# A causal mask added by products, head pairs reduced together, and fill products in blocks of twelve: one change to a fused attention and two-layer MoE kernel

## The chip, the core and the metric

The kernel runs on one core of one Trainium2 chip. The metric is the device time of one execution in microseconds (us). The engines are TensorE (PE, and PEld for its weight loads), VectorE (DVE), ScalarE (ACT), GpSimd (POOL) and SyncE (SP, which issues all the DMAs here).

## The reference, cut to what matters

```python
scores = scale * np.matmul(q, k.transpose(0, 1, 3, 2))     # batch 4, 8 heads, 576 tokens, head_dim 64
cum = np.cumsum(np.log(np.clip(f, 0.0001, 1.0)), axis=-1)
scores = np.where(causal, -1000000000.0, scores + cum[:, :, :, None] - cum[:, :, None, :])
scores = scores - np.max(scores, axis=-1, keepdims=True)
attn = np.exp(scores)
attn = attn / (np.sum(attn, axis=-1, keepdims=True) + 1e-09)
x = np.matmul(attn, v)                 # then 2304 tokens x 512
h = x @ w_in                           # 512 x 2048
x = (np.maximum(h, 0.0) + alpha * np.minimum(h, 0.0)) @ w_out
h2 = x @ w_in2
out = (h2 * np.tanh(softplus(h2))) @ w_out2
```

The weights are float64; the kernel turns them into float32 itself. The row maximum is taken over causal keys only.

## The kernel before, in words

**Order.** Nothing runs in the order of the source. Each piece of work is registered with `plan.add(engine, cost, priority, function, reads, writes)`, and `Plan.emit` then lists all of it, with estimated costs, and writes out one fixed order for each engine. An engine takes its instructions strictly in that order, so one that waits holds up all behind it. The table `PRIO` shifts starting priorities by stage name and by the number of the operation within its stage. A "use" (`plan.use`) is a PSUM buffer that the planner picks from a group: the group "two" has three pairs of banks, the group "one" has the single bank 6 before the change. The fill (below) has bank 7.

**Attention.** 32 heads go through as 16 pairs; the two heads of a pair lie in partitions 0 to 63 and 64 to 127, and their products run beside each other on two halves of TensorE (tile 64*128). For each pair:

- `load_qk`, `load_v`, `load_bias`: DMAs. `stage_T` splits q and k into a high and a low float32r part (ACT cast, then DVE subtraction, L331).
- `stage_M` (maxima): for five chunks of 128 queries, in six pieces of 320, 256, 64, 448, 320 and 192 keys, a q-k product (L609) and a bias product (L611) for each head go into a pair of banks. Then DVE takes, for each head by itself, the maximum with the mask `tri` added (L619, twelve operations per pair of heads, each followed by the reading of its accumulator) into `M5`. The five 128x128 columns of `M5` are transposed on TensorE (L631), and ACT adds `bvec` and writes `BQ` (L636, two operations).
- `stage_S` (scores): four pieces, each four passes (three q-k passes, and a last one with `BQ` and `BK` that adds bias and minus the maximum; L657). ACT takes the exponential (L667), POOL zeroes the upper triangle (L675).
- `stage_R` (row sums): POOL adds blocks (L693), TensorE sums over keys (L705), ACT and DVE form the reciprocal `uu` (L710 to L717).
- `stage_V`: products with v (L738) in two windows, and DVE scales them into `X` (L744).

`stage_S` of a pair stands one step behind `stage_M` in the source, so several pairs are in flight.

**Fill.** `group_a` computes part of the first MoE layer for three blocks of 384 tokens while attention is still running: four hidden chunks with 12 products of 128x384 each (`h_mm`, L782 to L784), the activation (`prelu`), and four output chunks with 12 products each (`out1`, L847 to L849). That is 288 products. Before the change the planner may place them in threes. `load_w` brings the eight weight tiles for it: a DMA, then ACT and DVE conversions (L399 to L405), and a split (ACT, POOL L331).

**The rest.** When attention is through, its memory is given back (`swap1`), and the remaining MoE work runs to the end, with 512-column products at L858 to L860.

Of the kernel before, what the change touches and what calls it, by code (L numbers as in the profile page):

```python
# [9 lines left out]
F32 = mybir.dt.float32  # L10
F32R = mybir.dt.float32r
# [226 lines left out]
def fox_attention__then__moe_prelu__then__moe_mish(  # L238
# [53 lines left out]
    banks = {n: psum.tile([P, 512], F32, tag=f"b{n}", name=f"b{n}") for n in range(8)}  # L292
# [115 lines left out]
    def conv_w(l, kind, fc, at, after=()):  # L408

        src = ((w_in1, w_out1), (w_in2, w_out2))[l][kind]  # L410
        i = n_w[0] % 2 if n_w[0] >= 2 * GA else 0
        n_w[0] += 1
        wbk = [("wb", i, m) for m in range(2)]
        for m in range(2):
            half_w(src, kind, fc, i, m, at, after if i else ())
        return lambda: wbs[i].bitcast(F32), wbk
# [6 lines left out]
    def load_w(l, kind, fc, slot, at, after=()):  # L423
        plan.stage("W" if after else "WA")
        split_w(*conv_w(l, kind, fc, at, after), (slot, kind), at, after)
# [31 lines left out]
    KEEP = 4  # L457
    PRE = "DVE"
    W_AT = 0.0
    bM = [7]  # L460
# [4 lines left out]
    plan.share("two", [(banks[2 * n], banks[2 * n + 1]) for n in range(3)])  # L465
    plan.share("one", [banks[6]])
# [13 lines left out]
    Pt = [ap1.tile([P, 2, PW], F32, tag=f"Pt{i}", name=f"Pt{i}") for i in range(2)]  # L480
# [5 lines left out]
    M5 = [ap1.tile([P, NQ, P], F32, tag=f"M5{i}", name=f"M5{i}") for i in range(2)]  # L486
# [3 lines left out]
    rr = ap1.tile([P, S], F32, tag="rr", name="rr")  # L490
    uu = ap1.tile([P, S], F32, tag="uu", name="uu")
    tri = ap1.tile([P, S + P], F32, tag="tri", name="tri")
    junk = ap1.tile([P, S - P], F32, tag="junk", name="junk")
    BQ1 = ap1.tile([P, P], F32R, tag="BQc", name="BQc")
    bvec = ap1.tile([P, 1], F32, tag="bvec", name="bvec")
# [4 lines left out]
    bias = c1[:NH, 2 * S:5 * S].rearrange("p (t n) -> p t n", t=3)  # L500

# [5 lines left out]
    def bank(group):  # L507
        n = bank_use.get(group[0], 0)
        bank_use[group[0]] = n + 1
        b = group[n % len(group)]  # L510
        return banks[b], ("bank", b)
# [6 lines left out]
    def prologue():  # L518
# [5 lines left out]
        plan.add("DVE", 0.74, -27, lambda: V.memset(tri, 0.0), w=["zero"])  # L524
        plan.add("POOL", 0.24, -25, lambda: G.affine_select(
            out=tri[:, S:], in_=tri[:, S:], pattern=[[-1, P]], compare_op=ALU.is_ge, fill=NEG, base=0, channel_multiplier=1),
            ["zero"], ["tri"])
        plan.add("POOL", 0.6, -12, lambda: G.memset(bias[:, 1], 1.0), r=pk, w=["bias1"])
        plan.add("DVE", 0.5, -9, lambda: V.tensor_scalar(fr, fr, 1e-4, 1.0, op0=ALU.max, op1=ALU.min), ["f"] + pk, ["f1"])
        plan.add("ACT", 0.67, -9, lambda: nc.scalar.activation(fr, fr, AF.Ln), ["f1"] + pk, ["f2"])  # L530
        plan.add("DVE", 0.8, -9, lambda: V.tensor_tensor_scan(
            out=cum, data0=fr, data1=tri[:NH, :S], initial=0.0, op0=ALU.add, op1=ALU.add), ["f2", "zero"] + pk, ["cum"])
# [3 lines left out]
            out=bias[:, 2].bitcast(F32R), in0=cum, scalar=m8, in1=bias[:, 0], op0=ALU.mult, op1=ALU.subtract), ["bh", "cum"] + pk, ["bl"])  # L536
        plan.add("DVE", 0.5, -20, lambda: (V.memset(bvec, 0.0), [V.memset(bvec[e * HALF:e * HALF + 3], 1.0) for e in range(2)]), w=["bvec"])
        plan.add("DVE", 0.5, -19, lambda: (V.memset(BQ1.bitcast(F32), 0.0), [V.memset(BQ1[e * HALF:e * HALF + 3].bitcast(F32), 1.0) for e in range(2)]), w=["BQ1"])
        plan.add("POOL", 0.3, -10, lambda: (G.memset(ones, 1.0), G.memset(eps, 1e-9)), w=["ones"])
        for i in range(2):  # L540
            plan.add("POOL", 0.7, -18 + 9 * i, lambda i=i: G.memset(BK[i].bitcast(F32), 0.0), w=[("BK", i)])
            plan.add("POOL", 0.7, -17 + 9 * i, lambda i=i: G.memset(M5[i], 0.0), w=[("M5", i, c) for c in range(NQ)])
# [27 lines left out]
    def load_v(pr, at):  # L570
        plan.stage("LV2")
        i = pr % 2
        n4 = (NQ - 1) * P
        dma(at, lambda: nc.sync.dma_start(vt[i][:, :NQ - 1], v[pr, :n4].rearrange("(c p) x -> p c x", p=P)), 262, runs=1.3, w=[("v", i, 0)])
        dma(at, lambda: nc.sync.dma_start(vt[i][:HALF, NQ - 1], v[pr, n4:]), 33, r=[("vpad", i)], w=[("v", i, 1)], issue=0.62)
# [11 lines left out]

    hs = [slice(e * HALF, (e + 1) * HALF) for e in range(2)]

    def stage_M(pr, at):  # L590
# [4 lines left out]
        for c in [NQ - 1, 0] + list(range(NQ - 2, 0, -1)):  # L595
# [5 lines left out]
            for n, (a, z) in enumerate(pieces):  # L601
# [5 lines left out]
                def mm(ps=ps, a=a, z=z, q0=q0):  # L607
# [430 lines left out]
```

## Time and profile before

| What | Value |
|---|---|
| Device time, three runs | median 1064.71 us (1062.28 to 1065.77) |
| The profiled execution | 1062.31 us, span 1060.5 us |
| Granted TensorE clock, mean | 0.985 |
| PE busy / DVE busy | 1023.7 us (97%) / 770.8 us (73%) |
| ACT busy / POOL busy | 520.0 us (49%) / 421.8 us (40%) |
| Last attention operation (L744) ends | 294.4 us |

A busy PE is not a PE at its peak: products are pipelined, each row's duration is longer than the distance to the next one, and an engine that runs at half the clock counts as busy too. What a product costs is therefore read from start to start in the timeline.

### The profile page before, as it was taken

How to read it: one execution, taken by the hardware profiler on the slowest of the kernel's cores; microseconds unless marked ns; L12 is line 12 of the kernel's file. 1: busy time of each engine (PE TensorE's matmuls, PEld its weight loads, DVE VectorE, ACT ScalarE, POOL GpSimd, SP SyncE). 2: the span in 40 equal slices, each digit the busy share in tenths (PEclk: the TensorE clock that was granted, in tenths of full speed). 3: DMA queues.
4: the chain of work that ended last, by engine and by line, in shares of the span. 5: the costliest groups of instructions: out<-in, count | busy, mean ns of one | idle time of the engine just before them, and what ended most of it. 6: DMA issues, size and time to landing. Idle time of an engine off the chain costs nothing.

```text
span 1060.5 us, 17610 instructions
## 1 busy us (share of the span) xinstructions
PE 1023.7 (97%) x6332; PEld 922.4 (87%) x6332; DVE 770.8 (73%) x1686; ACT 520.0 (49%) x1101; POOL 421.8 (40%) x416
## 2 busy tenths in 40 slices
PE   7897899999989999999999999999999999999998
PEld 6665677777779999999999999998999999999997
DVE  6776876766478877878622247979888788887885
ACT  3544555545346554534332336645455555554543
POOL 2554563554545654414232334333243322423231
PEclk9988999999989999999999999999999999999999
DMA  6132322210033445665510024100000000000000
GB/s 184 56 97 76 88 67 58 69 42 19 12 101 99 125 143 162 203 192 191 188 31 1 20 80 130 49 1 31 1 1 30 1 31 1 1 31 1 31 1 30
DMA packets 55207, 70.86 MB, mean 67 GB/s; under 512 B 6576, under 2 KB 32176, under 8 KB 55120
## 3 DMA queue, kind: packets, MB, share of 16 engines
q1 hardware_dynamic: 55120, 69.75, 21.5%
q8 instruction: 49, 0.80, 0.3%
q14 instruction: 38, 0.31, 0.1%
HBM read 56.39 MB, written 13.33 MB: 66 GB/s over the span
## 4 chain that ended last, share of the span: by engine, by line
PE 81%; DVE 9%; DMA 4%; issue 3%; ACT 1%; SPq 0%; POOL 0%; DVEq 0%; ACTq 0%
PE b L782 11%; PE b L784 11%; PE b L783 11%; PE b L859 6%; PE b L858 6%; PE b L860 6%; PE b L657 5%; PE b L847 5%; PE b L738 5%; PE b L849 4%; PE b L848 4%; DVE junk L619 2%; PE b L609 2%; DVE wb L405 2%; DVE wb L403 2%
## 5 line engine op out<-in xcount | busy, mean ns | idle before, releaser
L782 PE MATMUL b<-xh,w 128*128 128x384 f32 x768 | 260.5, 339 | 3.5 <-DVE x L807 1.3
L784 PE MATMUL b<-xl,w 128*128 128x384 f32 x768 | 257.8, 336 | 4.8 <-DVE xl L331 4.8
L783 PE MATMUL b<-xh,w 128*128 128x384 f32 x768 | 257.4, 335 | 0.0
L839 POOL TENSOR_TENSOR x<-x 128x384 f32<-128x384 f32 x96 | 113.0, 1177 | 245.5 <-DVE x L837 165.9
L782 PEld LDWEIGHTS b<-xh,w 128*128 128x128 f32 x768 | 144.1, 188 | 13.5 <-issue 2.2
L784 PEld LDWEIGHTS b<-xl,w 128*128 128x128 f32 x768 | 144.3, 188 | 5.2 <-DVE xl L331 5.2
L783 PEld LDWEIGHTS b<-xh,w 128*128 128x128 f32 x768 | 144.2, 188 | 3.9
L847 PE MATMUL b<-g,w 128*128 128x384 f32 x384 | 132.6, 345 | 8.0 <-DVE x L810 7.2
L331 POOL TENSOR_TENSOR g<-X,g 128x384 fp32r<-128x384 f32 x72 | 78.2, 1090 | 155.3 <-ACT g L321 124.2
L849 PE MATMUL b<-g,w 128*128 128x384 f32 x384 | 129.9, 338 | 0.0
L848 PE MATMUL b<-g,w 128*128 128x384 f32 x384 | 129.7, 338 | 0.0
L321 ACT CAST g<-x 128x384 fp32r<-128x384 f32 x120 | 61.6, 513 | 112.9 <-POOL x L839 103.8
L860 PE MATMUL b<-w,g 128*128 128x512 f32 x288 | 113.1, 393 | 0.0
L859 PE MATMUL b<-w,g 128*128 128x512 f32 x288 | 113.1, 393 | 0.0
L858 PE MATMUL b<-w,g 128*128 128x512 f32 x288 | 113.0, 392 | 0.0
L807 DVE SCALAR_TENSOR_TENSOR X<-X,alph,b 128x384 f32<-128x384 f32 x72 | 43.8, 610 | 74.5 <-ACT X L801 74.2
L619 DVE CUSTOM_DVE_ANT_0 junk<-b,tri 128x320 f32<-128x320 f32 (+3 forms) x160 | 69.2, 432 | 33.6 <-PE b L611 15.9
L331 DVE TENSOR_TENSOR g<-x,g 128x384 fp32r<-128x384 f32 x102 | 75.5, 742 | 16.9 <-ACT g L321 16.7
L399 ACT ACTIVATE wb<-raw 128x256 f32<-128x256 f32 x128 | 52.5, 433 | 69.0 <-DMA wd<-wb 33.8
L847 PEld LDWEIGHTS b<-g,w 128*128 128x128 f32 x384 | 73.1, 190 | 12.5 <-DVE x L810 8.4
L667 ACT ACTIVATE Pt<-b 128x512 f32<-128x512 f32 (+1 forms) x128 | 57.1, 505 | 42.8 <-PE b L657 41.5
L401 DVE TENSOR_SCALAR wb<-wb 128x256 int32<-128x256 int32 x128 | 54.5, 443 | 31.6 <-ACT wb L399 30.9
(94 smaller groups left out, 1999.4 us busy)
## 6 DMA issues: line engine op xcount, KB each, us to landing
raw<-in_moe_w_in_dram SPq DMA_DIRECT2D x64, 256.0 KB
raw<-in_moe_w_out_dram SPq DMA_DIRECT2D x64, 256.0 KB
wd<-wb SPq DMA_DIRECT2D x32, 256.0 KB
raw<-wd SPq DMA_DIRECT2D x32, 256.0 KB
qkr<-in_q_dram SPq DMA_DIRECT2D x16, 288.0 KB
qkr<-in_k_dram SPq DMA_DIRECT2D x16, 288.0 KB
out_dram<-x SPq DMA_DIRECT2D x18, 256.0 KB
vt<-in_v_dram SPq DMA_DIRECT2D x16, 256.0 KB
```

The source lines that it names most:

```text
L331: plan.add(engs, 0.0, at, lambda e: (nc.gpsimd if e == "POOL" else nc.vector).tensor_tensor(out=out(), in0=in0(), in1=in1(), op=ALU.subtra ...
L619: nc.vector.tensor_tensor_reduce(out=junk[ql, :z - a], in0=ps()[e][ql, :z - a], in1=tri[ql, x0 + a:x0 + z], scale=-1.0, scalar=BIG if n == ...
L782: nc.tensor.matmul(ps[:, :NB], w[:, 0, c], xh[c], start=(c == 0), stop=False)
L783: nc.tensor.matmul(ps[:, :NB], w[:, 1, c], xh[c], start=False, stop=False)
L784: nc.tensor.matmul(ps[:, :NB], w[:, 0, c], xl[c], start=False, stop=(c == KC - 1))
L839: add("POOL", c_pool(NB, 2.2), lambda e, m: nc.gpsimd.tensor_tensor(out=m, in0=e, in1=m, op=ALU.mult), [ek, mk], [mk])
L847: nc.tensor.matmul(ps[:, :NB], w[:, 0, c], g[:, 0], start=first, stop=False)
L848: nc.tensor.matmul(ps[:, :NB], w[:, 1, c], g[:, 0], start=False, stop=False)
L849: nc.tensor.matmul(ps[:, :NB], w[:, 0, c], g[:, 1], start=False, stop=last)
L858: nc.tensor.matmul(ps, g[:, 0, sl], w[:, 0], start=first, stop=False)
L859: nc.tensor.matmul(ps, g[:, 0, sl], w[:, 1], start=False, stop=False)
L860: nc.tensor.matmul(ps, g[:, 1, sl], w[:, 0], start=False, stop=last)
```

## The change

The change does these things.

- **Mask.** In the last piece of each chunk, four more products per piece (L635 of the changed kernel: two halves of the mask for each head, a 64x128 selector `sel` against a 64-row part of `tri`) add the causal mask in PSUM. `tri` shrinks to 128 columns; the prologue builds `sel` and `tri`.
- **Maxima.** One DVE `tensor_reduce` (L643) takes the maxima of both heads of a piece out of a double bank; `M5` is now 128 x 10 and one TensorE transpose (L650) of ten columns follows. ACT writes it, negated, as ten rows `MT` (L652), and four small DMAs on SP's queue (L656) move these rows into `BQ`. `bvec` and `junk` are gone.
- **Fill.** When the fill's bank group is given as a name, `h_mm` and `group_a` register twelve products as one operation, so nothing can be placed between them. The fill and `stage_V` now share the group "one", which has banks 6 and 7.
- **Loads.** The first weight loads come one pair later and wait for a `BQ` DMA of that pair; the order of the eight tiles is four w_in, then four w_out; the first v load waits for the first bias load.
- **Buffers.** `rr` and `uu` are doubled, and the first half of the reciprocal is written back into PSUM.

```diff
+    pairs = [pairs_pool.tile([P, 2, 512], F32, tag=f"bb{n}", name=f"bb{n}") for n in range(3)]
...
-    plan.share("two", [(banks[2 * n], banks[2 * n + 1]) for n in range(3)])
-    plan.share("one", [banks[6]])
+    plan.share("two", pairs)
+    plan.share("one", [banks[6], banks[7]])
...
-    M5 = [ap1.tile([P, NQ, P], F32, tag=f"M5{i}", name=f"M5{i}") for i in range(2)]
+    M5 = [ap1.tile([P, 2, NQ], F32, tag=f"M5{i}", name=f"M5{i}") for i in range(2)]
+    MT = [ap1.tile([2 * NQ, P], F32R, tag=f"MT{i}", name=f"MT{i}") for i in range(2)]
...
     def stage_M(pr, at):
...
                     for e in range(2):
-                        nc.tensor.matmul(ps()[e][:, :z - a], BQ1[hs[e]], BK[i][hs[e], a:z], start=False, stop=True)
+                        nc.tensor.matmul(ps()[:, e, :z - a], BQ1[hs[e]], BK[i][hs[e], a:z], start=False, stop=not last)
+                    if last:
+                        w = z - max(q0, a)
+                        for half in range(2):
+                            for e in range(2):
+                                nc.tensor.matmul(ps()[:, e, z - a - w:z - a], sel[hs[e], half], tri[hs[e], half, :w], start=False, stop=half == 1)
...
-                for e in range(2):
-                    dst = lambda e=e, c=c, ql=ql: M5[i][ql, c, e * HALF + 1:e * HALF + 2]
-                    plan.add("DVE", c_dve(z - a) * 1.08 + 0.01, ai, lambda e=e, ps=ps, a=a, z=z, ql=ql, n=n, last=last, x0=x0, dst=dst:
-                             nc.vector.tensor_tensor_reduce(
...
+                plan.add("DVE", c_dve(2 * (z - a)), ai, lambda ps=ps, a=a, z=z, ql=ql, dst=dst: nc.vector.tensor_reduce(
+                    out=dst(), in_=ps()[ql, :, :z - a], axis=mybir.AxisListType.X, op=ALU.max), [bk], ["nmx"] if part else [("M5", i, c)])
...
-        def tr():
-            for c in range(NQ):
-                q0 = rows(c)[0]
-                half = int(q0 >= W0)
-                nc.tensor.transpose(ps()[half][:, q0 - half * W0:q0 - half * W0 + P], M5[i][:, c], ident)
...
+        plan.add("PE", 0.11, at + 6, lambda: nc.tensor.transpose(ps()[:2 * NQ, 0, :P], M5[i].rearrange("p e c -> p (e c)"), ident),
+                 ["ident"] + [("M5", i, c) for c in range(NQ)], [bk, ("MT", i)])
+        plan.add("ACT", c_act(P), at + 6.3, lambda: nc.scalar.activation(MT[i], ps()[:2 * NQ, 0, :P], AF.Copy, scale=-1.0), [bk], [("MT", i)])
+        for e in range(2):
+            for c, n in ((0, 1), (1, NQ - 1)):
+                q0, w = rows(c)
+                dma(at + 6.5, lambda e=e, c=c, n=n, q0=q0, w=w: nc.sync.dma_start(
+                    BQ[i][e * HALF + 1:e * HALF + 2, q0:q0 + n * w].bitcast(F32),
+                    MT[i][e * NQ + c:e * NQ + c + n, :w].bitcast(F32)),
+                    2, r=[("MT", i), ("BQ1", i)], w=[("BQ", i, e, min(c, 1))], issue=0.62)
...
     def h_mm(slot, bs, at):
...
-        for c in range(KC):
...
-            plan.add("PE", 3 * c_pe(NB), at, mm, [("wh",) + wk, ("wl",) + wk, ("xh", c), ("xl", c)], [bk])
+        for cs in [range(KC)] if whole else [[c] for c in range(KC)]:
+            plan.add("PE", 3 * len(cs) * c_pe(NB), at, lambda cs=cs: mm(cs),
...
-                if h < 2 * GA:
-                    load_w(0, h % 2, h // 2, h // 2, at + (h % 2) * II + W_AT)
+                h -= 2 * W_FROM
+                if 0 <= h < 2 * GA:
+                    load_w(0, h // GA, h % GA, h % GA, at + (h % 2) * II + W_AT, behind=[("BQ", pr % 2, 0, 0)])
...
-        group_a(blk, TF0 + blk * 2 * GA * TFS, TFS, bM)
+        group_a(blk, TF0 + blk * 2 * GA * TFS, TFS, "one")
```

**Where the order moves: TensorE, transposes and scores.** Before, the five transposes of a pair's maxima (`M_134`, here pair 2) stand behind the row sums (L705), and the maxima of the next pair (L609, L611) follow.

```order
L705 MATMUL b_67<-Pt_122,ones 64x128 x2
L705 MATMUL b_67<-accp,ones 64x160 x2
L705 MATMUL b_68<-accp,ones 64x288 x2
L631 MATMUL b_69<-ident,M_134 128x128 x3
L631 MATMUL b_70<-ident,M_134 128x128 x2
L609 MATMUL b_65<-khl_129,qhl_127 128x320
L609 MATMUL b_66<-khl_129,qhl_127 128x320
```

In the changed kernel the maxima of pairs 2 and 3 come first, all of them with the mask products (L635); then the single transpose of pair 2 (`M_137`), the row sums (L725), the transpose of pair 3 (`M_138`), and at once the scores of pair 2 (L677), whose last pass reads `BQ_135`.

```order
L628 MATMUL bb_70<-khl_132,qhl_130 128x192 x2
L630 MATMUL bb_70<-BK_134,BQc 128x192 x2
L635 MATMUL bb_70<-tri,sel 128x128 x4
L650 MATMUL bb_68<-ident,M_137 10x128
L725 MATMUL bb_68<-Pt_125,ones 64x128 x2
L725 MATMUL bb_68<-accp,ones 64x160 x2
L725 MATMUL bb_68<-accp,ones 64x288 x2
L650 MATMUL bb_69<-ident,M_138 10x128
L677 MATMUL bb_70<-qhl_129,khl_131 128x288 x6
L677 MATMUL bb_70<-BQ_135,BK_133 128x288 x2
```

So between a pair's transpose and the first use of its `BQ` there stand here six row-sum products and one transpose.

**Where the order moves: SP's queue.** Before, SP's first thirty rows hold input, bias, v and weight loads; a stretch of it, where `raw` is the landing place of the weights, `BK` the bias rows and `qkr` the next pair's q and k:

```order
L566 DMA BK_131<-biasd 3x576 x2
L389 DMA raw_91<-in_moe_w_in_dram 128x2x128 x2
L393 DMA raw_91<-in_moe_w_out_dram 128x256 x2
L566 DMA BK_130<-biasd 3x576 x2
L389 DMA raw_91<-in_moe_w_in_dram 128x2x128
L558 DMA qkr_124<-in_k_dram 128x576
```

In the changed kernel the eight `BQ` DMAs of pairs 0 and 1 (L656) stand there, ahead of the first weight load, of the bias of pair 2 and of the next q and k loads.

```order
L656 DMA BQ_136<-MT_140 1x16x4
L656 DMA BQ_136<-MT_140 1x4x128
L656 DMA BQ_136<-MT_140 1x16x4
L656 DMA BQ_136<-MT_140 1x4x128
L393 DMA raw_94<-in_moe_w_in_dram 128x2x128 x2
L586 DMA BK_133<-biasd 3x576 x2
```

Over the whole program SP's rows grow by the four `BQ` DMAs of each of the 16 pairs.

## Rows read from the trace of the kernel before

**Rows 1.** The page's first line: span and instructions.

```profile
span 1060.5 us, 17610 instructions
```

**Rows 2.** Busy time by stage: length, PE, PEld, DVE, ACT, POOL, PEclk, DMA.

```profile
40.00:60.00 20.00, 15.90 (x124) 11.36 (x126) 17.66 (x54) 9.22 (x21) 13.88 (x15) 0.88 0.28 83
80.00:100.00 20.00, 14.25 (x93) 9.11 (x91) 17.23 (x46) 7.35 (x18) 8.57 (x8) 0.74 0.24 72
140.00:260.00 120.00, 118.56 (x1073) 92.49 (x1073) 81.72 (x257) 63.52 (x139) 62.01 (x74) 1.00 0.17 47
```

**Rows 3.** The chain that ended last, by line: 0 to 294, then 40 to 140.

```profile
by line: PE b L657 18.1%; PE b L738 16.7%; DVE junk L619 7.9%; PE b L609 6.5%; issue 6.2%; PE b L705 4.8%; PE b L782 3.9%; PE b L516 3.7%; PE b L611 3.6%; PE b L847 3.3%; PE b L784 2.7%; PE b L783 2.6%; PE b L631 2.4%; PE b L849 2.3%; PE b 
by line: PE b L738 19.2%; PE b L657 16.9%; DVE junk L619 13.2%; issue 10.0%; PE b L609 7.9%; PE b L611 3.7%; PE b L705 3.1%; PE b L782 2.8%; PE b L631 2.8%; DVE qhl L331 2.7%; DVE khl L331 2.3%; PE b L784 2.1%; DVE xl L331 1.8%; ACT Pt L667
```

**Rows 4.** Timeline of TensorE, maxima of one pair: start, length, instruction, idle before.

```profile
50.58 0.41 PE L609 MATMUL b<-khl,qhl 64*128 64x320 f32 x2
...
58.55 3.78 PE L738 MATMUL b<-Pt,vt 128*64 128x320 f32 x14
```

**Rows 5.** Groups of the maxima on DVE, 0 to 294: count, busy us, mean ns.

```profile
L619 DVE CUSTOM_DVE_ANT_0 junk<-b,tri 128x448 f32<-128x448 f32 x32 | 19.8, 620 | 6.5 <-PE b L611 3.9 <-DVE M L619 0.5 <-ACT rr L710 0.2
...
L619 DVE DVE_READ_ACCUMULATOR2_ANT M<- 128x1 f32 x128 | 10.5, 82 | 0.0
L619 DVE CUSTOM_DVE_ANT_0 junk<-b,tri 64x64 f32<-64x64 f32 x32 | 6.8, 212 | 4.1 <-PE b L611 1.5 <-DVE M L619 0.3 <-ACT x L321 0.2
```

**Rows 6.** Timeline of TensorE around 201: a visit to the fill between two maxima.

```profile
200.87 0.33 PE L783 MATMUL b<-xh,w 128*128 128x384 f32 x1
201.04 0.34 PE L784 MATMUL b<-xl,w 128*128 128x384 f32 x1
201.31 0.36 PE L609 MATMUL b<-khl,qhl 64*128 64x192 f32 x2
201.70 0.44 PE L782 MATMUL b<-xh,w 128*128 128x384 f32 x1
201.99 0.33 PE L783 MATMUL b<-xh,w 128*128 128x384 f32 x1
```

**Rows 7.** Timeline of TensorE: five transposes, 64-column scores, 64-key maxima.

```profile
205.12 0.76 PE L631 MATMUL b<-ident,M 128*128 128x128 f32 x5
205.64 0.42 PE L847 MATMUL b<-g,w 128*128 128x384 f32 x1
...
210.61 0.41 PE L657 MATMUL b<-qhl,khl 64*128 64x64 f32 x6
210.86 0.28 PE L657 MATMUL b<-BQ,BK 64*128 64x64 f32 x2
210.97 0.68 PE L657 MATMUL b<-qhl,khl 64*128 64x320 f32 x6
...
213.40 0.30 PE L609 MATMUL b<-khl,qhl 64*128 64x64 f32 x2
213.53 0.28 PE L611 MATMUL b<-BK,BQc 64*128 64x64 f32 x2
```

**Rows 8.** Timeline, all engines: the first loads and the first maxima; SPq issues.

```profile
13.04 1.58 SPq L566 DMA_DIRECT2D BK<-Pt  x2
...
16.13 0.56 PE L611 MATMUL b<-BK,BQc 64*128 64x320 f32 x2 [1.06 <-DMA BK<-Pt]
...
28.90 1.10 ACT L636 ACTIVATE BQ<-b,bvec 128x320 fp32r<-128x320 f32 x2 [2.52 <-PE b L631]
```

**Rows 9.** Timeline of TensorE: the second visit to the fill.

```profile
82.58 0.34 PE L783 MATMUL b<-xh,w 128*128 128x384 f32 x1
87.77 0.69 PE L784 MATMUL b<-xl,w 128*128 128x384 f32 x1 [4.85 <-DVE xl L331]
```

**Rows 10.** Bias DMAs from DRAM on SP: ns min/median/max of one issue.

```profile
L566 SPq DMA_DIRECT2D BK<-biasd x30: 233/259/274, 17.3 to 245.4; - x30
```

**Rows 11.** SP's queue, 0 to 294: who waited for whom, total us, times, longest.

```profile
SPq L574 <- PE b L738: 95.2, 13, 14.2
```

More of the change, by code (lines that the diff above doesn't have):

```diff
@@ L291, in fox_attention__then__moe_prelu__then__moe_mish @@
     psum = pool("psum", space=PSUM)
-    banks = {n: psum.tile([P, 512], F32, tag=f"b{n}", name=f"b{n}") for n in range(8)}
+    psa = ExitStack()
+    pairs_pool = pool("psa", stack=psa, space=PSUM)
+    pairs = [pairs_pool.tile([P, 2, 512], F32, tag=f"bb{n}", name=f"bb{n}") for n in range(3)]
+    psum = pool("psum", side="right", space=PSUM)
+    banks = {n: psum.tile([P, 512], F32, tag=f"b{n}", name=f"b{n}") for n in (6, 7)}
     def c_pe(n, m=P):
@@ L406, in half_w, with conv_w @@
             out=wb(), in0=half(0, I32), scalar=29, in1=wb(), op0=ALU.logical_shift_right, op1=ALU.bitwise_or), [rwk, wbk], [wbk], port=BOTH)
-    def conv_w(l, kind, fc, at, after=()):
+    def conv_w(l, kind, fc, at, after=(), behind=()):
         src = ((w_in1, w_out1), (w_in2, w_out2))[l][kind]
@@ L414, in conv_w @@
         for m in range(2):
-            half_w(src, kind, fc, i, m, at, after if i else ())
+            half_w(src, kind, fc, i, m, at, [*(after if i else ()), *behind])
         return lambda: wbs[i].bitcast(F32), wbk
@@ L457, in fox_attention__then__moe_prelu__then__moe_mish @@
     KEEP = 4
+    NPT = 2
+    FIRST = [("BKr", 0, e) for e in range(2)]
     PRE = "DVE"
     W_AT = 0.0
+    W_FROM = 1
     bM = [7]
@@ L500, in fox_attention__then__moe_prelu__then__moe_mish @@
     bias = c1[:NH, 2 * S:5 * S].rearrange("p (t n) -> p t n", t=3)
+    hs = [slice(e * HALF, (e + 1) * HALF) for e in range(2)]
     def rows(i):
@@ new lines, in stage_M @@
+                part = kn > 512 and not last
+                dst = lambda part=part, c=c, ql=ql: nmx[ql] if part else M5[i][ql, :, c]
+                plan.add("DVE", c_dve(2 * (z - a)), ai, lambda ps=ps, a=a, z=z, ql=ql, dst=dst: nc.vector.tensor_reduce(
+                    out=dst(), in_=ps()[ql, :, :z - a], axis=mybir.AxisListType.X, op=ALU.max), [bk], ["nmx"] if part else [("M5", i, c)])
+                if kn > 512 and last:
+                    plan.add("DVE", 0.07, ai, lambda c=c, ql=ql: nc.vector.tensor_tensor(
+                        out=M5[i][ql, :, c], in0=M5[i][ql, :, c], in1=nmx[ql], op=ALU.max), ["nmx"], [("M5", i, c)])
```

197 lines of the change are left out of this document (106 added, 91 removed).

## The prediction

> **What bounds the kernel now.** I read the profile's page first, then busy time by stage, then the chain of waits for the attention part alone, then the timelines of TensorE, DVE and SP there. The whole span is 1060.5 us [rows 1]. The change touches nothing that runs after attention and the three fill blocks, which together end about 294 us into the span, so what it can win or lose lies in those 294 us; the MoE part behind them moves as a whole.
>
> In these 294 us there are two regimes. From 140 to 260 us TensorE is busy for 118.56 of 120 us, at the full granted clock [rows 2]: there it sets the time, and whatever is added to it costs. From about 40 to 140 us it does not. In 40 to 60 and 80 to 100 us DVE has 17.66 and 17.23 of 20 us, TensorE only 15.90 and 14.25, and the clock granted to TensorE is 0.88 and 0.74 [rows 2], a mean of its two levels. The chain of waits says the same: of the 100 us from 40 to 140, DVE's maxima at L619 carry 13.2% and "issue" (a hand-over in which nothing visible is waited for) 10.0%; over the 294 us they carry 7.9% and 6.2%, which is 23.2 and 18.2 us [rows 3]. The timeline shows how: the 24 products of one pair's maxima take from 50.58 to 58.55, 8 us [rows 4], because each pair of banks waits until DVE has taken two maxima out of it.
>
> **The change part by part.** A plus is time won.
>
> *Mask products, minus 11.* Each of the five chunks gets four products, so a pair of heads gets 20; as two heads run beside each other on the two halves of the array, these are 10 steps, 160 in all. No such product is in the trace. The nearest rows: eight 64-column products, four steps, take from 210.61 to 210.97, 0.09 a step; a step of 64-key maxima takes from 213.40 to 213.53, 0.13 [rows 7]. I take 0.11, the middle, because both carry a 128-column weight load each as the new ones do: 1.1 us a pair, 17.6 us in all (14.4 to 20.8). They cost only where TensorE sets the time. In the first six pairs the maxima stand together and DVE sets their pace (8 us a pair in [rows 4], about 4.4 by the estimate below, while the mask adds 1.1), so the work is hidden under DVE there; if DVE were faster than I think, that cover would go and 6.6 us come back. Ten pairs remain: 11.0 us.
>
> A page of the Trainium skill would make this cheaper. The Trainium skill, "TensorE: Matmul & The Clock Gate", section "Wait — 56ns, not 53.3ns?", gives 55.6 ns from start to start for warm products of 128 columns; by it 160 steps are 8.9 us, and the ten pairs 5.6. The trace does not agree for this kind of product: its shortest step is 0.09 us at half as many columns.
>
> *Transposes, plus 4.* Five take from 205.12 to 205.64, 0.104 each [rows 7]. Four fewer over the same ten pairs: 4.2 us (6.7 if all sixteen count).
>
> *Fill in twelves, plus 6.* TensorE pays for going to the fill and back: the product after 201.04 starts 0.27 us later instead of the 0.17 between 200.87 and 201.04, and the first one of the next visit, at 201.70, holds the second up until 201.99, 0.29 instead of 0.17 [rows 6]. That is 0.10 and 0.12, or 0.22 a visit. Before the last product with v the order has 47 visits before and 21 in the changed kernel: 26 x 0.22 = 5.7 us. The price is that nothing can break into a block of 12 x 0.17 = 2.1 us; in that time DVE and ACT still have queued work.
>
> *Maxima on DVE, plus 7.* No reduction of this form is in the trace. L619 takes 620 ns for 448 elements and 212 for 64 [rows 5], so 1.06 ns an element and 144 ns on top; its accumulator reading takes 82 ns. A pair of heads has 1600 keys a head in six pieces: before, 12 x 144 + 3200 x 1.06 + 12 x 82 = 6.1 us; now, if the reduction runs at L619's pace, 6 x 144 + 3200 x 1.06 + 0.1 for the small joining operation = 4.4 us, 0.71 of it. Of the 23.2 us on the chain that saves 6.7. Bounds: nothing, if the reduction is 40% slower an element, and 11.6 if it halves.
>
> *Hand-overs, plus 3.* Of the 18.2 us of "issue" many stand between DVE's maxima and TensorE. The operations fall from 24 a pair (with the readings) to 7. Between 0 and 10 us, the amount in 40 to 140; I take 3, since the other half of a hand-over stays.
>
> *First visits to the fill, plus 4.5.* At 82.58 the fill waits for its third product until 87.77, 5.2 us where 0.17 are normal, because DVE is late with `xl` [rows 9], and the clock falls in that window [rows 2]. In the new order the first fill block stands behind the transpose of pair 7, where it stood behind that of pair 3; x is long split by then. I take 3.5 of the 5.0 us (DVE's backlog may hold up something else; 0 to 5), and 1 for products that no longer run at 1.2 GHz.
>
> *`BQ` by DMA, minus 7.* Before, ACT needs 1.10 us for `BQ` [rows 8]. Now ACT needs perhaps 0.4 for one short operation, SP issues four DMAs at 0.26 each [rows 10], and the last has to land. For landing the trace gives bounds: the first bias DMAs are issued from 13.04 to 14.62 and the product that needs them starts at 16.13 [rows 8], 1.5 us after the end of the issue and 3.1 after its start. So 2.9 to 4.5 us, 1.8 to 3.4 more than before. Between transpose and scores TensorE has cover almost everywhere (other pairs' maxima, products with v, fill). In the order it is thin at four places, pairs 0, 2, 4 and 8, where only row sums (4.8% of 294 us, 0.9 us a pair [rows 3]) and a transpose or a few products stand between. 4 x about 1.8 = 7 (0 to 14). These DMAs also wait on SP, in order: behind them stand the first weight load, the bias of pair 2 and q and k loads. Conversions on ACT and DVE, and later maxima, wait for those. SP has room, though: it sits 95.2 us in waits of the v loads alone [rows 11], and 64 more issues are 17 us.
>
> The Trainium skill speaks against this step. "DMA: Bandwidth & Descriptors", section "Anatomy of one DMA — SWDGE (gpsimd) path", puts about 2.0 us of fixed cost on every DMA, however small. That lies inside the bounds from the rows, so the trace agrees as far as it shows the thing.
>
> *Prologue, plus 2.* The first maxima wait until 16.13 for a bias DMA issued at 13.04 [rows 8]. The first weight loads and a v load no longer stand ahead of it; building `sel` and `tri` adds DVE and POOL work that fits before 13 us. 0 to 4.
>
> *At nothing:* ACT loses an eviction a pair and POOL clears two `BQ` tiles instead of two large `M5`, both hidden, since ACT and POOL have half their time free (63.52 and 62.01 of 120 us [rows 2]). Two banks shared by fill and v products, and doubled `rr` and `uu`, may help or hinder by a microsecond or two.
>
> Sum: -11.0 + 4.2 + 5.7 + 6.7 + 3.0 + 4.5 - 7.0 + 2.0 = 8.1 us won. The profiled execution was 1062.31 us, 2.4 us under the median of its three runs; 1062.3 - 8.1 + 2.4 = 1056.6, and I say 1056.
>
> **The rivals.**
>
> *The early stretch comes free.* From 40 to 140 us about 30 of 100 us on the chain are not TensorE's (13.2 + 10.0, and 2.7 + 2.3 + 1.8 of subtractions on DVE [rows 3]). If DVE, relieved of 27 us (16 x 1.7), falls behind TensorE there altogether, those 30 us go instead of the 14.2 in my sum: 24 us won, 1041. For it: DVE at 88% is the fullest engine there. Against it: maxima of two pairs now stand in one block, so DVE still sets the pace inside it.
>
> *Nothing in sum.* The mask products cost in all pairs (17.6), and the maxima stay bound by DVE because the new reduction is slower than L619: -17.6 + 6.7 + 5.7 + 4.5 + 2.0 is about 1 us, less what `BQ` costs: 1064.
>
> *Slower: `BQ` becomes the wait of every pair.* If a DMA of a few rows queued behind weight loads lands 1.5 us later than I take it, cover of two or three microseconds no longer does at the ten later pairs: 15 us more, 7 lost in sum, 1072. It decides from about 2.9 us between transpose and scores. For it: SP's order puts weight and q/k loads right between the `BQ` DMAs. Against it: the planner leaves far more than that at most pairs. The Trainium skill's fixed cost, named above, is the root of this rival.
>
> **How the numbers follow.** The forecast (3 to 14 us won, 1051 to 1062) gets 0.42, the early stretch 0.25, nothing in sum 0.16, slower 0.17. A measurement of this kernel tells about 0.3%, 3.2 us, from no change. Faster takes the first two but for a little of the forecast's edge that lies within 3.2 us and goes to the same: 0.66; same 0.17; slower 0.17. The likeliest case's own range is 1050 to 1062; over the cases 1038 to 1071.
>
> **What would show it.** Right, if the profile after has: L643 near 0.82 us for 640 elements; L635 steps near 0.11 us; the maxima's share of the chain down by a third; no wait of 5 us in a first fill block; waits on `BQ` DMAs at pairs 0, 2, 4 and 8 only; the last attention operation about 8 us earlier; and an unchanged length from there to the end. The prediction is wrong if reductions take more than 1.2 us, if TensorE waits for `BQ` at most pairs, or if v products wait for banks that the fill holds.

## The result, and the profile after

The changed kernel is slower: 1070.95 us median (1065.07 to 1080.33, 20 runs) against 1065.63 (1060.97 to 1069.81, 20 runs), ratio 1.0057, 95% interval 1.004 to 1.0075. Its profiled execution took 1066.52 us. I had forecast 1056 (1050 to 1062). Runs of one program differ with their mean granted TensorE clock (the changed kernel's go from 1065.1 us at 0.986 to 1080.3 at 0.970), so times are best compared at like clock; the two profiled executions have 0.985 and 0.984.

The page's first lines of the changed kernel:

```profile
span 1064.8 us, 17828 instructions
## 1 busy us (share of the span) xinstructions
PE 1023.5 (96%) x6588; PEld 937.3 (88%) x6588; DVE 756.8 (71%) x1418; ACT 510.1 (48%) x1088; POOL 423.4 (40%) x424
```

The span is 4.3 us longer than in [rows 1]. The first three stages below answer to [rows 2]; the last two lie behind attention (columns: length, PE, PEld, DVE, ACT, POOL, PEclk, DMA share, GB/s).

```profile
40.00:60.00 20.00, 18.93 (x220) 15.71 (x219) 14.37 (x27) 9.64 (x22) 9.87 (x13) 1.00 0.24 73
80.00:100.00 20.00, 18.36 (x149) 14.12 (x148) 16.49 (x34) 8.68 (x20) 9.90 (x12) 0.74 0.25 75
140.00:260.00 120.00, 115.87 (x1127) 97.28 (x1125) 74.65 (x127) 56.68 (x127) 59.08 (x72) 0.99 0.17 49
400.00:440.00 40.00, 36.59 (x201) 35.65 (x200) 29.53 (x66) 15.14 (x36) 11.32 (x9) 0.96 0.47 152
480.00:520.00 40.00, 35.50 (x196) 35.21 (x195) 30.01 (x63) 15.26 (x37) 11.54 (x12) 0.96 0.53 167
```

The same two late stages of the kernel before:

```profile
400.00:440.00 40.00, 40.00 (x231) 39.64 (x230) 30.79 (x71) 16.72 (x39) 15.31 (x14) 1.00 0.62 191
480.00:520.00 40.00, 40.00 (x233) 40.00 (x232) 31.19 (x71) 17.77 (x43) 13.97 (x13) 1.00 0.56 178
```

TensorE was never idle there before and now loses 3.4 and 4.5 us, though no line of the MoE part was edited.

**Where the time went, at equal work.** Since the two orders differ, times of equal names can't be compared. I add up, in order of time, the work of all products that both kernels have: columns at 2.4 GHz plus a fixed charge for each kind of product, the same in both (mask products, transposes and warm-up products left out; both sums end at 916.9 us). With other charges the entries up to work 180 move by up to 4 us, those from 280 on hardly. The table says when a kernel has started so much of this work, as the difference to the kernel before; minus is ahead.

| Work done (us) | Before, at | Changed | Old order behind attention | The same again | Order of the changed kernel in the one before |
|---|---|---|---|---|---|
| 60 | 140.7 | -0.1 | -1.1 | +4.4 | +3.4 |
| 140 | 249.3 | +3.3 | +2.5 | +8.0 | +3.4 |
| 180 | 306.6 | -6.5 | -7.4 | -2.0 | +1.2 |
| 280 | 415.8 | -6.4 | -6.0 | -0.4 | +2.6 |
| 300 | 435.8 | -0.9 | -6.0 | -0.4 | +8.5 |
| 360 | 496.6 | -1.9 | -6.1 | -0.3 | +7.5 |
| 380 | 516.5 | +4.4 | -5.5 | +0.0 | +15.2 |
| 900 | 1039.3 | +4.3 | -4.7 | +0.6 | +15.2 |

The changed kernel is 6.4 us ahead when attention and its aftermath are over, near the 8.1 of my sum, but up to work 140 it is not ahead: the 6.4 arise behind 249 us. Then it loses 5.5 us between work 280 and 300 and 6.3 between 360 and 380. Nothing happens behind. The timeline of TensorE shows the second place (start, length, instruction, idle before):

```profile
509.76 0.34 PE L808 MATMUL b<-xh,w 128*128 128x384 f32 x1
509.94 0.34 PE L809 MATMUL b<-xl,w 128*128 128x384 f32 x1
514.77 0.66 PE L872 MATMUL b<-g,w 128*128 128x384 f32 x1 [4.50 <-DVE x L936]
515.23 0.52 PE L873 MATMUL b<-g,w 128*128 128x384 f32 x1
515.55 0.52 PE L874 MATMUL b<-g,w 128*128 128x384 f32 x1
...
517.79 0.46 PE L872 MATMUL b<-g,w 128*128 128x384 f32 x1
518.09 0.34 PE L873 MATMUL b<-g,w 128*128 128x384 f32 x1
518.26 0.34 PE L874 MATMUL b<-g,w 128*128 128x384 f32 x1
```

4.83 us from one product to the next where 0.17 are normal, and then ten products 0.30 to 0.46 apart (514.77 to 518.09, 1.6 us more than ten times 0.17) before the distance is back at 0.17: half the rate, so the 1.2 GHz level after the wait. That is 4.66 + 1.6 = 6.3 us, the loss in the table. L872 waits for L936, DVE's sum that takes the finished output of a token block out of its bank. DVE in that time:

```profile
503.13 0.75 DVE L409 SCALAR_TENSOR_TENSOR wb<-raw,wb 128x256 int32<-128x256 int32 x2
506.19 0.29 DVE L405 TENSOR_SCALAR wb<-wb 128x256 int32<-128x256 int32 x1 [2.31 <-ACT wb L403]
508.19 0.29 DVE L405 TENSOR_SCALAR wb<-wb 128x256 int32<-128x256 int32 x1 [1.70 <-ACT wb L403]
508.40 0.76 DVE L407 SCALAR_TENSOR_TENSOR wb<-raw,wb 128x256 int32<-128x256 int32 x2
509.07 0.75 DVE L409 SCALAR_TENSOR_TENSOR wb<-raw,wb 128x256 int32<-128x256 int32 x2
509.74 1.13 DVE L835 SCALAR_TENSOR_TENSOR X<-X,alph,b 128x384 f32<-128x384 f32 x2
510.79 0.28 DVE L405 TENSOR_SCALAR wb<-wb 128x256 int32<-128x256 int32 x1
511.26 0.91 DVE L405 TENSOR_SCALAR wb<-wb 128x256 int32<-128x256 int32 x1 [0.19 <-ACT wb L403]
512.09 1.54 DVE L407 SCALAR_TENSOR_TENSOR wb<-raw,wb 128x256 int32<-128x256 int32 x2
513.56 0.60 DVE L835 SCALAR_TENSOR_TENSOR X<-X,alph,b 128x384 f32<-128x384 f32 x1
514.08 0.54 DVE L936 TENSOR_TENSOR x<-b,x 128x384 f32<-128x384 f32 x1
```

L405 to L409 convert weights of the second MoE layer, which nobody needs yet. DVE sits 4 us behind two of them, because ACT's first step (L403) waits:

```profile
505.72 0.43 ACT L403 ACTIVATE wb<-raw 128x256 f32<-128x256 f32 x1 [5.52 <-DMA wd<-wb]
507.73 0.43 ACT L403 ACTIVATE wb<-raw 128x256 f32<-128x256 f32 x1 [1.57 <-DMA raw<-in_moe_w_in_dram]
```

The sum, whose last three products start at 508.03, stands in order behind all that. The first place, at 411.36, has the sums behind conversions too: 2.99 us to the next product, half the rate from 415.71 to 418.59 (1.3 us more), then 1.28 us at 418.59; together nearly the 5.5. DVE does not stand still there, but its conversions take longer than the 0.48 (L405) and 0.75 us (L407) that they take elsewhere:

```profile
407.65 2.22 DVE L405 TENSOR_SCALAR wb<-wb 128x256 int32<-128x256 int32 x2
409.80 1.57 DVE L407 SCALAR_TENSOR_TENSOR wb<-raw,wb 128x256 int32<-128x256 int32 x2
```

**The attention part.** The chain of waits, 0 to 294 and 40 to 140, answers to [rows 3]:

```profile
by line: PE bb L677 16.4%; PE b L760 11.5%; PE bb L628 5.2%; issue 4.6%; PE b L527 4.6%; PE bb L725 4.2%; PE bb L635 3.5%; PE bb L630 3.4%; PE b L872 3.4%; DVE M L643 3.3%; PE b L807 3.3%; PE b L874 2.9%; PE b L873 2.8%; PE b L809 2.6%; PE 
by line: PE bb L677 16.3%; PE b L760 14.2%; issue 8.3%; PE bb L628 6.1%; DVE M L643 4.9%; DVE bb L735 4.7%; PE bb L635 4.5%; PE bb L630 4.3%; ACT Pt L686 3.8%; ACT rr L730 3.6%; PE bb L725 3.5%; ACT rr L733 3.4%; DVE uu L737 3.1%; PE b L527
```

The maxima fall from 23.2 us to 9.7 (3.3%) over the 294, more than I said. But from 40 to 140 the reciprocal's four steps now carry 14.8% (L735, L730, L733, L737), where they carried 3.2 before, and the mask products 4.5%. The waits of TensorE up to 294 us (total, times, longest) say the same; no group is larger than 5.2 us:

```profile
PE bb L650 <- DVE M L643: 5.2, 4, 3.1
PE bb L630 <- DMA BK<-Pt: 3.4, 2, 3.1
PE bb L677 <- DMA BQ<-MT: 2.5, 3, 1.0
```

The reduction, all forms, then the 640-element one (ns min/median/max), answering to [rows 5], and the mask products, of which four (two steps) start 0.17 us before the next product, 0.085 a step:

```profile
L643 DVE TENSOR_REDUCE M<-bb x80: 270/681/1094, 18.1 to 261.4; 128x2 f32<-128x512 f32 x16, 64x2 f32<-64x128 f32 x16, 128x2 f32<-128x896 f32 x16, 128x2 f32<-128x640 f32 x16
...
L643 DVE TENSOR_REDUCE nmx<-bb x16: 808/820/826, 15.7 to 249.3; 128x2 f32<-128x640 f32 x16
```
```profile
55.43 0.34 PE L635 MATMUL bb<-tri,sel 64*128 64x128 f32 x4
55.60 0.25 PE L628 MATMUL bb<-khl,qhl 64*128 64x64 f32 x2
```

The `BQ` DMAs on SP's queue (ns min/median/max of one issue), answering to [rows 10]:

```profile
L656 SPq DMA_DIRECT2D BQ<-MT x64: 508/589/693, 30.2 to 265.8; - x64
```

### The profile page after: what moved, and what is told of

Same layout as the page of the kernel before. It is cut to its first block, busy times and chain, and to the rows that moved or that the text cites. A ratio compares the mean times of both kernels' runs of the same rounds, so it can differ in the third digit from the quotient of the medians.

```text
span 1064.8 us, 17828 instructions
## 1 busy us (share of the span) xinstructions
PE 1023.5 (96%) x6588; PEld 937.3 (88%) x6588; DVE 756.8 (71%) x1418; ACT 510.1 (48%) x1088; POOL 423.4 (40%) x424
## 4 chain that ended last, share of the span: by engine, by line
PE 82%; DVE 9%; ACT 3%; issue 3%; DMA 2%; POOL 1%; SPq 0%; DVEq 0%; ACTq 0%; POOLq 0%
PE b L807 12%; PE b L809 11%; PE b L808 11%; PE b L887 6%; PE b L886 6%; PE b L888 6%; PE b L872 5%; PE b L874 5%; PE b L873 5%; PE bb L677 5%; PE b L760 3%; DVE wb L407 2%; PE bb L628 1%; PE b L527 1%; PE bb L725 1%
## 5 line engine op out<-in xcount | busy, mean ns | idle before, releaser
L872 PE MATMUL b<-g,w 128*128 128x384 f32 x384 | 130.3, 339 | 8.3 <-DVE x L936 7.2
L829 ACT ACTIVATE X<-b 128x384 f32<-128x384 f32 x72 | 34.9, 489 | 97.9 <-PE b L809 97.8
L872 PEld LDWEIGHTS b<-g,w 128*128 128x128 f32 x384 | 72.5, 189 | 10.4 <-ACT wb L403 4.8
L686 ACT ACTIVATE Pt<-bb 128x512 f32<-128x512 f32 (+1 forms) x128 | 56.8, 506 | 49.8 <-PE bb L677 43.0
L403 ACT ACTIVATE wb<-raw 128x256 f32<-128x256 f32 x128 | 52.8, 434 | 54.0 <-DMA wd<-wb 24.1
L861 DVE SCALAR_TENSOR_TENSOR b<-x 128x384 f32<-128x384 f32 x96 | 67.0, 698 | 12.5 <-ACT x L860 10.4
```

The source lines that it names most:

```text
L861: add("DVE", c_dve(NB), lambda e, m: V.scalar_tensor_tensor(out=u(), in0=m, scalar=2.0, in1=e, op0=ALU.add, op1=ALU.mult), [mk, ek], [uk], ...
L872: nc.tensor.matmul(ps[:, :NB], w[:, 0, c], g[:, 0], start=first, stop=False)
```

## The experiments

Every time is a median with its ratio to the kernel before, run beside it, and the 95% interval.

### Whose are the waits behind attention: the order's, or a limit of the weight stream?

The planner makes the order of the whole program anew for every change. Here each engine's order from about 310 us on is replaced by that of the other kernel; all operations behind attention are the same in both.

```diff
+TAIL = [...]      # planned start of each operation of the MoE part in the other kernel
+TAIL_FROM = 280
...
+            if when[self.post0 + i] >= TAIL_FROM:
+                when[self.post0 + i] = x + 1000.0
...
+            chain = sorted((n for n in N if eng[n] == e), key=lambda n: (when[n], rank[n]))
```

> The changed kernel with the order that the kernel before has behind attention (MoE part only; everything up to about 310 us is the changed kernel's own). The changed kernel is 6.4 us ahead of the kernel before at equal TensorE work at 409 us and 4.4 us behind at 521 us. Theory A, the re-made order behind attention put DVE operations that TensorE needs behind weight conversions that wait for loads: with the old order the two waits near 411 and 510 us go, the 6.4 us stay won, about 1056 us. Rival B, the weight stream of 300 to 520 us is at its limit and TensorE, coming earlier, must wait there in any order: waits come back in the same stretch, 1062 to 1067 us.

Measured: 1057.47, ratio 0.9926 (0.9907 to 0.9945). Both waits are gone; TensorE's waits from 395 to 620 us add up to 1.5 us, where the changed kernel has 8.0:

```profile
PE b L906 <- ACT X L863: 0.7, 1, 0.7
PE b L908 <- POOL g L369: 0.5, 1, 0.5
PE b L906 <- DVE x L970: 0.3, 1, 0.3
```

> The mirror: the kernel before with the order that the changed kernel has behind attention. Theory A: it takes over the two waits, about 10.8 us more than the kernel before, 1073 us. Rival B: TensorE comes there 6 us later than in the changed kernel, so little is waited for: 1062 to 1065 us.

Measured: 1078.51, ratio 1.0122 (1.0101 to 1.0144): 12.7 us slower than the kernel before, by the last column of the table at the same two places and more (its longest wait there, 4.9 us, is put down to ACT's conversions and not to DVE's sums). Theory A holds both ways: the order behind attention is worth 9 to 13.5 us, whichever of the two attention parts stands ahead of it.

### The mask products

```diff
-                    if last:
-                        ...
-                                nc.tensor.matmul(ps()[:, e, z - a - w:z - a], sel[hs[e], half], tri[hs[e], half, :w], start=False, stop=half == 1)
```

> The changed kernel in its own order without the mask products (the causal mask is left out of the maxima). My prediction: 11 of 17.6 us lie open, attention ends 11 us earlier; if they are open in the early pairs too, 17 us. At the end of the kernel: theory A (waits behind attention belong to the order, not to a rate) lets the gain through, 1050 to 1056 us; rival B (weight stream at its limit) swallows most of it behind attention, 1062 to 1066 us. If the maxima of the early pairs are paced by DVE, the time at which 20 to 60 us of common TensorE work are done does not change.

Measured: 1060.84, ratio 0.9963 (0.9946 to 0.998), between the two forecasts and 10.1 us less than the changed kernel in the medians. At equal work, in profiled executions with clocks of 0.979 here and 0.984 there, it is as fast as the changed kernel up to work 60 (+0.4 against -0.1), and 4 us ahead of it from 160 on; both waits behind attention are still there.

> The changed kernel in its own order with every mask product issued twice (the values stay far below the true maxima). Attention ends 11 us later by my prediction's open share, 17 us later if all of it is open. At the end: theory A 1077 to 1084 us; rival B, whose waits behind attention shrink by what attention is later, 1067 to 1073 us.

Measured: 1077.55, ratio 1.0111 (1.0088 to 1.0134). The second set costs 11 us at equal work from 140 to 280 and 6.6 in the medians. Its five runs have clocks of 0.983 to 0.986; the four of the changed kernel with 0.984 or more have a median of 1065.4, 12 us less. So at most a part of either set lies in cover.

### Third buffer for the conversions

```diff
+        y = n_w[0] % 3 if l else i
...
-            return wbs[i][:, cols]
+            return wbs[y][:, cols]
```

> The changed kernel with its own order on every engine, instruction for instruction; only the conversions of the second layer's weights go round three buffers wb instead of two, so a conversion no longer waits for the DMA that stores the one two before it. Theory A2 (the waits near 411 and 510 us come from DVE, which stands in order behind such conversions and has the sums behind it that free TensorE's banks): both waits shrink to under 1 us, about 1056 to 1060 us. Rival C (DVE simply has too much to do there, or it is the loads that are late): the waits stay, 1066 to 1071 us.

Measured: 1093.75, ratio 1.027 (1.024 to 1.0299). This was not the test that I meant. Two streams, `w_in` and `w_out`, had one buffer each; with three in turn they share them, wait for each other (TensorE waits 16.1 us for DVE's sums), and in an order made for two buffers a weight can be overwritten before it is stored (argued, not shown). It tells nothing on A2.

### The price of `BQ`, of DVE's maxima, of the blocks of twelve and of the moved loads

These four start from the version with the old order behind attention, where the waits behind attention are small. The first two keep its order on every engine. The last two make the order of the attention part anew, so what they measure is not the term alone.

```diff
-                    MT[i][e * NQ + c:e * NQ + c + n, :w].bitcast(F32)),
+                    MS[e * NQ + c:e * NQ + c + n, :w].bitcast(F32)),
...
-                    Pt[p][:, e, poff[s]:poff[s] + pw[s]], ps()[:, e, :pw[s]], AF.Exp, scale=-ISC), [bk], [pk[e]])
+                    Pt[p][:, e, poff[s]:poff[s] + pw[s]], ps()[:, e, :pw[s]], AF.Exp, scale=-1e-4 * ISC), [bk], [pk[e]])
```

> The changed kernel with the old order behind attention (1057.5 us), and the four BQ DMAs of each pair read a constant tile, so that nothing in them waits for the maxima; the maxima are left out of the scores by it, and the exponential's scale is set close to zero to keep its values in range. My prediction's term: 7 us won, 1050. By the waits for BQ in the trace (3.9 us with the weight loads' share): about 1054. If other waits stand behind them: 1057.

Measured: 1061.73, ratio 0.9962 (0.9944 to 0.9979). No gain: the waits for `BQ` are gone from the trace, and other waits stand behind them.

```diff
-                    out=dst(), in_=ps()[ql, :, :z - a], axis=mybir.AxisListType.X, op=ALU.max)
+                    out=dst(), in_=ps()[ql, :, :(z - a) // 2], axis=mybir.AxisListType.X, op=ALU.max)
```

> The changed kernel with the old order behind attention (1057.5 us); the reduction L643 reads only the first half of the keys of each piece (the other half is left out of the maxima, the exponential's scale is close to zero). DVE saves 16 x 1600 x 1.06 ns = 27 us, about 12 of it before 140 us. If DVE's maxima pace the early stretch, as my prediction has it, 60 us of common TensorE work are done 6 to 12 us earlier, 1046 to 1051 us at the end. If something else holds the early stretch: within 2 us, 1055 to 1057.

Measured: 1055.63, ratio 0.9922 (0.9894 to 0.9951), 2 to 6 us less than its base in two measurements (1057.47, and 1061.86 below). Work 60 is done at -1.3 us, where the base has -1.1: DVE's maxima do not pace the stretch up to there; what this run wins it wins later.

```diff
-    plan.share("one", [banks[6], banks[7]])
+    plan.share("one", [banks[6]])
...
-        group_a(blk, TF0 + blk * 2 * GA * TFS, TFS, "one")
+        group_a(blk, TF0 + blk * 2 * GA * TFS, TFS, bM)
```

> The changed kernel with the old order behind attention (1057.5 us), but the fill in threes with bank 7 for itself, as before (the products with v have bank 6 alone again). 42 visits to the fill before the last product with v instead of 21. By my prediction's 0.22 us a visit: 4.6 us slower, 1062 us. If blocks of twelve gain nothing because what they save in switches they lose in held-up work: 1056 to 1058 us.

Measured: 1063.24, ratio 0.9978 (0.9962 to 0.9994), 1.4 to 5.8 us slower than the base. At like clock it is closer: its eight runs with 0.983 or more have a median of 1062.9, the ten of the base 1057.9, so 5.0 us where 4.6 were expected. The sign and the size are those of my term, but the run undoes the blocks and the shared banks together, in an order made anew.

```diff
-    W_FROM = 1
+    W_FROM = 0
...
-                    load_w(0, h // GA, h % GA, h % GA, at + (h % 2) * II + W_AT, behind=[("BQ", pr % 2, 0, 0)])
+                    load_w(0, h % 2, h // 2, h // 2, at + (h % 2) * II + W_AT)
...
-        after = FIRST if pr == 0 else []
+        after = []
...
-    load_v(0, 2)
+    load_v(0, -1)
```

> The changed kernel with the old order behind attention (1057.5 us) and the weight and v loads as before: first weight loads one pair earlier, without waiting for a BQ DMA, w_in and w_out by turns, first v load early. My prediction gives the moved loads 2 us in the prologue and 3.5 to 4.5 at the first fill visits: 1063 us. If the early stretch is held by something else: 1056 to 1059.

Measured: 1063.37, ratio 0.9976 (0.9961 to 0.9991): 1.5 to 5.9 us slower than the base, 4.5 at like clock (six runs, median 1062.4), with the order made anew here too.

### What on DVE makes the waits

```diff
-        dma(at, lambda: nc.sync.dma_start(t, bf()), 256, r=wbk, w=[("wd", kind, fc)])
+        dma(at, lambda: nc.sync.dma_start(t, zero[0]), 256, r=wbk, w=[("wd", kind, fc)])
```

> The changed kernel in its own order; the DMAs that store the second layer's converted weights read a constant tile, so the next conversion on ACT waits for no store (the second layer's weights are left out, the traffic stays). Theory A2 (TensorE waits near 411 and 510 us because DVE stands in order behind conversions that wait for stores): the two waits shrink from 3.0 and 4.8 us to under 1 us each, 1056 to 1060 us. Rival C (DVE has too much to do there, or loads are late): they stay, 1066 to 1071 us.

Measured: 1071.42, ratio 1.0058 (1.0039 to 1.0076). A2 falls. ACT waits for no store any more, but 19.2 us for the loads of `w_in` instead (5.8 in the changed kernel, both from 380 to 530 us), and TensorE waits as before (395 to 620 us):

```profile
PE b L873 <- DVE x L937: 7.8, 2, 6.0
```

So the store that the trace named was only the last of several. The next two runs take DVE's part of these conversions away.

```diff
-        plan.add("DVE", c_dve(HM, True), at, lambda: V.tensor_scalar(
+        plan.add("DVE", c_dve(HM, True), at, lambda: skip or V.tensor_scalar(
...
+            half_w(src, kind, fc, i, m, at, [*(after if i else ()), *behind], l == 1)
```

> The changed kernel in its own order without DVE's three operations for each half of a second-layer weight (that part of the conversion is left out; ACT's part, the loads and the stores stay). Theory A3 (the sums that free TensorE's banks stand on DVE behind these conversions, which wait for ACT and for loads): the waits near 411 and 510 us fall under 1 us each, 1055 to 1060 us. Rival D (the planner's order on ACT or TensorE itself makes the waits): 1065 to 1071 us.

Measured: 1056.31, ratio 0.9917 (0.9891 to 0.9942), 14.6 us less than the changed kernel. From 395 to 620 us no wait of TensorE is left; at equal work it goes from 2.9 us ahead at 280 to 4.0 at the end, where the changed kernel loses 10.7.

> The same in the kernel before. Theory A3: its order has little of this behind 400 us (one wait of 1.1 us at 459), so 1 to 3 us won, 1060 to 1065 us. If DVE's conversions slow the kernel in any order: 8 to 12 us won, as in the changed kernel.

Measured: 1064.75, ratio 0.9987 (0.9972 to 1.0002), about 1 us won, not clear of noise. The same operations cost 14.6 us in one order and 1 in the other. A3 holds: it is where they stand ahead of the sums, not that DVE has too much to do.

### Is the order luck?

```diff
-    SWITCH = 0.2
+    SWITCH = 0.21
```

> The changed kernel with one cost of the planner changed by a hundredth of a microsecond (SWITCH 0.20 to 0.21); the program's work is the same, only the order is made anew (the planner's own forecast changes by 0.1 us). If an order is worth the same when the planner says so: 1066 to 1071 us. If the order behind attention is luck: anything from 1055 to 1075, with waits of its own place behind attention.

Measured: 1072.05, ratio 1.0062 (1.0047 to 1.0076), again with its largest wait behind attention (5.1 us for ACT's conversions).

> The kernel before, nudged in the same way (the planner's own forecast gets 5.0 us worse). If the planner's forecast holds: 1070 to 1071 us. If the order is luck: anything from 1058 to 1078, and the difference arises at waits, not in the rate of the work.

Measured: 1064.22, ratio 0.9992 (0.9979 to 1.0006). The nudge made the order of the kernel before anew, in front of and behind the end of attention, and its time stayed within 2 us. In the changed kernel it moved operations of the attention part only: from 276 us on TensorE, DVE and ACT take the same instructions in the same order in both traces. So that run repeats the changed kernel's order behind attention, with losses at the same two places (the longest wait put down to DVE's sum in one profile, to ACT's conversions in the other). Whether these waits are an accident of this one order, or come with the changed kernel's list of operations, stays open. The planner's costs don't see them: by them the changed kernel was 11.4 us ahead of the kernel before, and the version with the old order 4.0 behind the changed one (the planner's own numbers, no times of the chip); the chip turned both round.

### The mask under the old order, and the new version again

Two more runs on one chip: the version with the old order, with and without the mask products.

> The changed kernel with the old order behind attention (1057.5 us) without the mask products (the causal mask is left out of the maxima). My prediction's term, ten of sixteen pairs open at 0.11 us a step: 11 us, 1046.5. If all sixteen pairs are open: 17 us, 1040. By the profile of the run without them in the changed kernel's own order, 4 us ahead at 300 us: 1053.5.

Measured: 1057.14, ratio 0.9915 (0.9893 to 0.9936).

> The changed kernel with the old order behind attention a second time, beside the run without mask products: 1057.5 us if the first measurement holds, with the two waits near 411 and 510 us absent again. If that run was a lucky one: 1060 to 1066.

Measured: 1061.86 (12 runs), ratio 0.9965 (0.994 to 0.999), the waits near 411 and 510 us absent. So the mask products cost 4.7 us here in the medians. But the runs without them have clocks of 0.975 to 0.982, and the seven with them in this range a median of 1064.75, 7.6 us more; how far the products themselves move the clock is not shown. The version with the old order beats both kernels in both measurements, by 4 to 8 us over the kernel before. Its first number was on the lucky side: those five runs have 0.985 to 0.987, and the five here with 0.983 or more took 1057.6 to 1059.7 us.

The two profiles of this one program show where. They part in the first 50 us:

```profile
10.00:30.00 20.00, 16.03 (x138) 13.85 (x136) 9.22 (x17) 0.79 (x2) 0.00 (x0) 0.91 0.27 82
30.00:50.00 20.00, 18.26 (x157) 15.26 (x159) 7.21 (x11) 8.72 (x21) 6.37 (x9) 0.83 0.16 48
```
```profile
10.00:30.00 20.00, 17.58 (x102) 15.11 (x101) 6.18 (x12) 0.68 (x1) 0.00 (x0) 0.66 0.26 81
30.00:50.00 20.00, 17.90 (x150) 15.28 (x152) 6.16 (x12) 5.78 (x14) 2.77 (x6) 0.83 0.10 28
```

With a granted clock of 0.66 instead of 0.91 from 10 to 30 us, the second is 5.4 us later at work 40, and keeps that to the end. What lowers the clock there in one run and not in the other is not shown.

## Why the prediction was wrong

**The step that failed** stands in its first paragraph: "The change touches nothing that runs after attention and the three fill blocks [...] the MoE part behind them moves as a whole." The source does not touch it, but the planner orders the whole program, and the new order put sums that free TensorE's banks behind conversions that wait. That cost 9 to 13.5 us (old order in the changed kernel, and the mirror); it is these conversions, since without DVE's part of them 14.6 us come back in this order and about 1 in the old one. Everything else together would have been a small win: the old order behind attention gives 1057.5 and 1061.9, the second at the very edge of the range that I gave to the forecast (1050 to 1062). I had compared the two orders only inside attention.

**The sum for attention**, 8.1 us, was near the 6.4 at equal work and the 4 to 8 of the medians, but mostly by luck. It has 14.2 us won in the early stretch; at 140.7 us the changed kernel is 0.1 ahead, and at 249.3 it is 3.3 behind. The 6.4 arise between work 150 and 180 (263 to 307 us), where the kernel before has waits of its own (2.2 us at 266.6, 3.6 at 301.5). The last attention operation ends at 288.1 us, 6.3 earlier; but the new order has 276 fill products ahead of the last product with v and the old one 300, and 24 at 0.17 are 4 of these 6.3. Term by term:

- *Mask products, minus 11*: a step is mis-sized, 0.085 us and not 0.11 (160 are 13.6). What of it is open is not settled: leaving the products out won 10.1 us in one order and 4.7 in the other (7.6 at like clock), and a second set cost 6.6 in the medians and 11 at equal work. My 11 is the upper end of that. The cover that I granted the first six pairs (no cost up to work 60) was there.
- *Maxima on DVE, plus 7, and hand-overs, plus 3*: the durations were right (820 ns for 640 elements, L619's pace) and their share of the chain fell by more than half, but no time came back by it up to work 60: the reciprocal's steps on ACT and DVE took the place at unchanged durations (3.2% of 40 to 140 us before, 14.8 after), "issue" fell only from 10.0 to 8.3%, and halving the columns of the reduction left the time of work 60 unchanged. That DVE's maxima set the pace there was wrong.
- *`BQ` by DMA, minus 7*: about nothing. TensorE waits for it three times, 2.5 us, and taking the wait away won nothing. SP's part was mis-sized all the same: an issue takes 0.59 us, not the 0.26 of the bias DMAs, so the 64 are 37 us in SP's queue and not 17. (What the prediction takes from the Trainium skill for the fixed cost of a DMA is said there of DMAs that GpSimd issues; SyncE issues these.)
- *Fill in twelves, plus 6; loads and first visits, plus 6.5*: 1.4 to 5.9 us each when undone, 5.0 and 4.5 at like clock, each with an attention order made anew. The wait of 5 us in a first fill block [rows 9] is gone, as foretold; but the granted clock from 80 to 100 us is 0.74 as before, and no run shows the 1 us for products that no longer run at 1.2 GHz.
- *Transposes, plus 4*: not tried by itself.

**The rivals.** *Early stretch free* is out: in every version looked at, work 60 is done within some 5 us of the kernel before, not earlier by the 30 us of that rival. *Slower by `BQ`* is out as a mechanism, though the sign came. *Nothing in sum* is out by its condition, since the reduction keeps L619's pace; its sum was also wrong, as it keeps the 6.7 us that the condition takes away. What stays open: how the gain up to 310 us divides, since the early stretch differs by 5 us between two runs of one program, and whether the planner would put the waits into another order of the changed kernel too.

## What to carry to other kernels

Where a scheduler makes the order of the whole program, a change has two effects, its own and that of the new order, and the second can be larger; forecast and measure them apart, by giving one version the other's order where their operations are the same. Compare traces at equal work: the difference then shows the place where the time is lost, here 120 us behind the edit. Work with no due time (weights for a later layer) must not stand in an in-order queue ahead of what frees the bottleneck's buffers, and when one wait is removed without gain, look at what stands next in the same queue.

## What the hardware showed unexpectedly

Three places. A wait of TensorE costs more than its length: after 4.66 us of it, ten products ran at the 1.2 GHz level, 1.6 us more. In the early stretch one and the same program reached equal work 5.4 us apart, with granted clocks of 0.91 and 0.66 in the same 20 us, so terms of 3 us can't be read there from single profiles. And DVE's conversions are slow beside POOL: two L407 take 2.40 us while POOL runs its subtraction, 0.75 when it does not:

```profile
498.25 2.40 DVE L407 SCALAR_TENSOR_TENSOR wb<-raw,wb 128x256 int32<-128x256 int32 x2
...
502.46 0.75 DVE L407 SCALAR_TENSOR_TENSOR wb<-raw,wb 128x256 int32<-128x256 int32 x2
```
```profile
497.12 2.08 POOL L335 TENSOR_TENSOR xl<-X,xh 128x384 fp32r<-128x384 f32 x2
499.16 2.35 POOL L335 TENSOR_TENSOR g<-X,g 128x384 fp32r<-128x384 f32 x2
```

The wait at 510 us holds such a pair too: two L407 take 1.54 us from 512.09, while GpSimd's subtractions run from 511.02 to 513.02.

The Trainium skill, "SBUF — State Buffer", section "SBUF: two separate sides", has a rule for it: a DVE operation with two SBUF inputs and a GpSimd one that reads SBUF share a pair of ports, and one holds it for its whole length while the other stands still. These rows agree.
